# A top-k attention and PReLU MLP kernel: where the copy of an output block and the transposes of q and k stand in their queues

## The chip, the cores and the metric

The kernel runs on one core of one Trainium2 chip. The metric is the device time of one execution in microseconds (us). A core has five engines, each with a queue of its own that it works off in order: TensorE (PE in the profile), VectorE (DVE), ScalarE (ACT), GpSimd (POOL) and SyncE (SP, which only issues DMAs here). They wait for each other through semaphores.

## The reference: what is computed

For 8 batches of 8 heads, with 576 rows of 64 numbers each, attention is computed in which each row keeps only its 32 largest scores:

```python
scores = scale * np.matmul(q, k.transpose(0, 1, 3, 2))
kth = np.partition(scores, -32, axis=-1)[..., -32:-31]
scores = np.where(scores >= kth, scores, -1e9)
attn = np.exp(scores - np.max(scores, axis=-1, keepdims=True))
attn = attn / (np.sum(attn, axis=-1, keepdims=True) + 1e-09)
x = np.matmul(attn, v)            # then (B, S, H*D) -> (4608, 512)
h = x @ w_in                      # (512, 2048)
g = np.maximum(h, 0.0) + alpha * np.minimum(h, 0.0)
out = g @ w_out                   # (2048, 512)
```

q, k, v, weights and output are float32. The output is 4608 rows of 512: 36 blocks of 128 rows.

## The kernel before, in words

**Units of work.** Heads are handled in 32 pairs, 4 pairs a batch. The rows of scores are cut into 144 duos: a duo is two tiles of 128 rows by 576 scores (lines 77 to 85). A batch is 18 duos: 16 of kind "n" (a tile of each head of a pair) and 2 of kind "m" (the last 64 rows of the heads, put together). The main loop (line 722) has one slot for each duo and 4 more to drain. Everything in flight is shifted against the duo whose scores are made: in slot n

- PE makes the scores of duo n+1 into the only `ps_sc` buffer (`st_qk`, line 233), and the products of attention weights and v for duo n-7 into `xo` (`st_av`, line 429);
- ACT runs two Sign passes with counts for duo n-2 (`sg`, `st_count`), Exp for duo n-5 (`w`, `st_exp`), two Relu passes for duo n-4 (`r`, `st_relu`), and copies the scores of duo n+1 from `ps_sc` to `s_sb` (`st_exit`, line 255), which frees `ps_sc`;
- POOL multiplies scores by signs (`y`), then subtracts the Relu result from the scores (`s_sb<-s_sb,r`), and casts v;
- DVE takes the largest 8 of six groups a row (12 instructions `up` and `small`), every second slot folds them into a threshold `p`, takes row maxima of `y` into `p`, picks the threshold for Relu (`KZ`), and normalises `xo` (a reciprocal into `KZ`, then `x`);
- SP transposes the weights of Exp by DMA (`wT<-w`) and issues the loads and stores.

**The MLP** is spread over the slots. When 128 or 256 transposed tokens (`xT`) are there, units of h are put into a list (`mlp_ready`, line 510). A unit (`h_pe`, line 547) is 8 or 16 products into `ph`; DVE turns it into `gT` with a maximum (`h_dve`, line 566). The linear share of the activation is handled by a weight matrix `w_lin_b` made once (the "lin" items of slots 16 to 23). An output block of 128 tokens is four parts (`part`, line 532), numbered 0 to 3, of one product with `w_lin_b` and four with `w_out_b`, all into the only `pz` buffer. `o_pe` (line 572) issues the next part, but only when no finished block waits for its copy (`not stores`). Part 3 puts the block on `stores`, with the first slot in which it may be copied: `now[0] + late_o[0]`. `o_act` (line 577) is the copy `o_sb<-pz` on ACT; the DMA to memory is issued by SP at the beginning of the next slot (`o_sp`, line 591; by POOL in three slots of the drain).

**q and k of later pairs** are loaded to staging buffers, transposed on PE in three units (`prep_pe`, line 186): four 128x128 transposes of k, four of q, and two of the tails of both, into a `tps` buffer. `tps`, `ph` and the filler products share a pool of two buffers (`ps_h`, tag "h"). The transposes are copied to `qkT` at the end of the slot (lines 767 to 771): the wide ones of k, in even slots, on DVE, those of q, in odd slots, on ACT, the tails on DVE. From pair 4 on, a pair's three units stand in three slots that follow each other, and the fourth slot has none.

**The order in a slot** is written by hand; the engines keep the order of the program. On PE in slot n: a unit of h or, if there is none, four filler products on an idle tile (`keep_warm`, `rest<-idle`, line 560); scores of duo n+1; av; a part of a block (line 745); in some even slots a second unit of h; transposes (line 756); then a second part if more than two are ready (line 763), or a filler if no part ran. On ACT: Sign twice, Exp, Relu twice, the copy of the scores, then `o_act` (line 758), then the copy of q's transposes. `o_act` runs if the kernel is in the drain, if more than 4 parts are ready, or if only short copies of transposes are pending in this slot. `late_o` is 1 only around the second part (line 762 to 766): a block that ends in the first part of a slot may be copied in that same slot, one that ends in the second part in the next.

The helper at line 32 records every instruction, so the profile gives "L32" for all of them; they are told apart by the names of their tiles.

Of the kernel before, what the change touches and what calls it, by code (L numbers as in the profile page):

```python
# [59 lines left out]
def fast_path(tc, q, k, v, moe_w_in, moe_w_out, moe_alpha, out, flag):  # L60
# [27 lines left out]
    with ExitStack() as ctx:  # L88
# [89 lines left out]
        todo, now = {}, [0]  # L178
# [5 lines left out]
        pend = []  # L184
# [44 lines left out]
        def two_of(ap, step, m):  # L229

            return bass.AP(ap.tensor, ap.offset, [list(ap.ap[0]), [step, 2], [1, m]])

        def st_qk(n):

            d = duos[n]
            ps = ps_s.tile([128, 1536], FP32, name="ps_sc", tag="s")
            T["ps", n] = ps
            if d[0] == "n":  # L240
                _, p, j = d
                t = qkT[p]
                c = slice(128 * j, 128 * j + 128)
                PE.matmul(ps[:, 0:512], t[0:64, 1, c], t[0:64, 0, 0:512], start=True, stop=True)
                PE.matmul(ps[:, 1024:1536], t[64:128, 1, c], t[64:128, 0, 64:S], start=True, stop=True)
                PE.matmul(two_of(ps[:, 512:1024], 448, 64), t[:, 1, c],
                          kds[p % len(kds)].rearrange("p (a b) -> p a b", a=2), start=True, stop=True)
                return
            for i, o, n0, n1 in ((0, 0, 0, 512), (1, 960, 64, S), (0, 0, 512, S), (1, 960, 0, 64)):
                t = qkT[d[1 + i]]  # L250
                for h in range(2):
                    r = slice(64 * h, 64 * h + 64)
                    PE.matmul(ps[r, o + n0:o + n1], t[r, 1, 512:S], t[r, 0, n0:n1], start=True, stop=True)

        def st_exit(n):
            s = s_p.tile([128, 2, S], FP32, name="s_sb", tag="s")
            ACT.copy(s, two_of(T.pop(("ps", n)), 960, S))
            T["s", n] = s
# [119 lines left out]
        def duos_at(kind, n):  # L378
            return stage.get((kind, n), [])
# [15 lines left out]
        def st_count(n):  # L395
            s, p9 = T["s", n], T["p9", n // 2]
            sg = two.tile([128, 2, S], BF16, name="sg", tag="sg", bufs=3)
            if n % 2 == 0:
                T["cs", n // 2] = three.tile([128, 4], FP32, name="cs", tag="cs")
            cs = T["cs", n // 2]  # L400
            for i in range(2):
                r = 2 * (n % 2) + i
                ACT.activation(sg[:, i, :], s[:, i, :], AF.Sign, bias=p9[:, r, 0:1], scale=-1.0,
                               accum_out=cs[:, r:r + 1])
            T["sg", n] = sg
# [16 lines left out]
        def st_exp(n):  # L422
            w = ws[n % 3]
            ACT.activation(w[:, :, 0:S], T.pop(("s", n)), AF.Exp, scale=att_scale)
            wt = three.tile([128, 10, 128], BF16, name="wT", tag="wT")
            SP.dma_start_transpose(wt, w.rearrange("p a b -> p (a b)"))
            T["wt", n] = wt

        def st_av(n):
            d = duos[n]  # L430
            wt = T.pop(("wt", n))
            if n % 2 == 0:
                T["xo", n // 2] = ps_x.tile([128, 2, 2, 65], FP32, name="xo", tag="x")
            xo = T["xo", n // 2][:, n % 2, :, :]
            for i in range(2):
                if d[0] == "n":
                    p = d[1]
                    for c in range(5):
                        K = 128 if c < 4 else 64
                        PE.matmul(xo[:, i, :], wt[0:K, 5 * i + c, :], v1[p][0:K, c, i, :],  # L440
                                  start=(c == 0), stop=(c == 4))
                else:
                    p = d[1 + i]
                    for h in range(2):
                        for c in range(5):
                            K = 128 if c < 4 else 64
                            PE.matmul(xo[64 * i:64 * i + 64, h, :], wt[0:K, 5 * i + c, 64 * h:64 * h + 64],
                                      v1[p][0:K, c, h, :], start=(c == 0), stop=(c == 4))
# [59 lines left out]
        soon, hq, oq, act, stores, late_o = [], [], [], [], [], [0]  # L508
# [38 lines left out]
        def h_pe(most=1):  # L547
            while soon and soon[0][0] <= now[0]:
                hq.append(soon.pop(0)[1])
            if hq and wi_free and len(act) < most:  # L550
                hq.pop(0)()
                return True

        def ready():
            k = 0
            while lin_done and k < len(oq) and oq[k][0]["done"] >= oq[k][1]:
                k += 1
            return k

        def keep_warm():  # L560

            ps = ps_h.tile([128, 512], FP32, name="rest", tag="h")
            for i in range(4):
                PE.matmul(ps, idle[:, 0:128], idle, start=(i == 0), stop=(i == 3))
# [7 lines left out]
        def o_pe():  # L572
            if ready() and not stores:
                oq.pop(0)[2]()
                return True

        def o_act():

            if stores and stores[0][3] <= now[0]:
                z, t0, pieces, _ = stores.pop(0)  # L580
                o = io.tile([128, DMODEL], FP32, name="o_sb", tag="io")
                ACT.copy(o, z)
                at, left = 0, []
                for r0, m in pieces:
                    if t0 <= at < t0 + 128:
                        left.append((r0, at - t0, m))
                    at += m
                outs.append((o, left))
        outs = []

        def o_sp():
            while outs:
                o, left = outs.pop(0)
                for r0, p, m in left:
                    (POOL if now[0] in (ND + 1, ND + 2, ND + 3) else SP).dma_start(out[r0:r0 + m, :], o[p:p + m, :])
# [74 lines left out]
        def run(n, kind, most=99):  # L670
            l = todo.get((n, kind), [])
            for f in l[:most]:
                f()
            if l[most:]:
                todo.setdefault((n + 1, kind), [])[0:0] = l[most:]
# [46 lines left out]
        for n in range(ND + 4):  # L722
            end = n >= ND
            now[0] = n
            run(n, "ld")
            o_sp()

            if end:
                for m in duos_at("av", n):
                    st_av(m)  # L730
            if not h_pe() and not end:
                keep_warm()
            if n and on(n + 1):
                st_qk(n + 1)
            if not end:
                for m in duos_at("av", n):
                    st_av(m)
            late = len(hq) > (9 if n < 118 else 4) and n % 2 == 0 or end

            for m in duos_at("count", n):  # L740
                st_count(m)
                st_y(m)
            for m in duos_at("exp", n):
                st_exp(m)
            did = o_pe()
            run(n, "w")

            dve_slot(n, late)
            for m in duos_at("relu", n):
                st_relu(m, 0)  # L750
                st_relu(m, 1)
            if on(n + 1):
                st_exit(n + 1)
            run(n, "cast")
            run(n, "lin_out")
            run(n, "prep", 2 if n < 4 else 1)
            if end or ready() > 4 or all(len(d.shape) == 3 for d, _ in pend):
                o_act()
            if (n, "lin") in todo:
                run(n, "lin")  # L760
            else:
                late_o[0] = 0 if end else 1
                if not (end or ready() > 2) or not o_pe():
                    if not end and not did:
                        keep_warm()
                late_o[0] = 0
            while pend:
                short = len(pend[0][0].shape) == 3
                wide = pend[0][0].shape[1] == 512
                on_dve = short and n > 16 or wide and (n < 17 or n % 2 == 0)  # L770
                prep_evac(DVE.tensor_copy if on_dve else ACT.copy)
            if n == 1:
                sm(DVE.tensor_copy(alpha_ps, aps), [], [(304, 320)])
                ACT.activation(alpha1m, aps, AF.Copy, scale=-1.0, bias=1.0)
            run(n, "scale")
            if norm_of(n):
                st_xT(norm_of(n) - 1)
                st_xT(norm_of(n))
            if n == ND + 3:
                check_low()  # L780
# [294 lines left out]
```

## Time and profile before

| | |
|---|---|
| median of 3 runs | 869.93 us (868.83 to 876.24) |
| the profiled execution | 875.8 us, of which the span from first to last instruction is 873.7 us |
| mean granted clock of PE | 0.956 |
| busy: PE, DVE, ACT, POOL | 773.5, 763.8, 766.2, 755.4 us |
| loop, 121 to 813 us: busy DVE, ACT, POOL | 642.7, 645.1, 639.8 of 692 us |

In a row of the timeline the first number is the start in us from the span's start, the second the duration; then follow engine, line, operation, the tile written, the tile read, shapes and the number of instructions merged. Brackets at the end give the idle time of the engine just before, and what ended it. Durations on one engine overlap a little, as instructions are pipelined, so the step from one start to the next is what counts. A row of the waits gives: who waited, for whom, us in total, how many times, the longest. A row of the table by stage gives the stretch, its length, the busy time and instructions of PE, PEld (weight loads), DVE, ACT and POOL, the granted clock of PE as a share of full speed, the busy share of the DMA engines and GB/s.

### The profile page before, as it was taken

The page shows a single profiled execution, that of the slowest core. Times are in us where ns is not written, and L with a number is a line of the kernel's source. Part 1 is how long each engine was busy: PE and PEld are TensorE (multiplying, and loading weights), DVE is VectorE, ACT ScalarE, POOL GpSimd, SP SyncE. Part 2 cuts the span into 40 slices and gives each one's busy share as a digit, 9 for nine tenths or more (in the row PEclk, how much of TensorE's full clock was granted, in tenths as well). Part 3 has the DMA queues.
Part 4 walks back from the last instruction along what each step waited for, and adds up shares of the span by engine and source line. Part 5 has one row for each costly group of instructions (what it writes and reads, how often), then busy time and mean ns, then how long its engine had stood idle before and what let it go on. Part 6 is the DMA issues. An engine that isn't in the chain of part 4 may idle for free.

```text
span 873.7 us, 17781 instructions
## 1 busy us (share of the span) xinstructions
PE 773.5 (89%) x5386; PEld 434.0 (50%) x5386; DVE 763.8 (87%) x3475; ACT 766.2 (88%) x1255; POOL 755.4 (86%) x708
## 2 busy tenths in 40 slices
PE   8778799989988989899978999989879889899887
PEld 5333345555545555455544555555445555455454
DVE  4879889999998999989998898999897889999732
ACT  4789999999997999989998899999997888999830
POOL 2789989999997898989997898999897987999930
PEclk9979899999999999989989999999998999999989
DMA  7599976555564455545555455556756554344341
GB/s 145 145 174 171 170 140 133 114 115 104 130 125 102 100 118 118 113 112 104 130 117 110 103 110 119 116 125 119 124 107 112 109 93 96 77 91 77 79 97 41
DMA packets 344167, 100.19 MB, mean 115 GB/s; under 512 B 338032, under 2 KB 338048, under 8 KB 344064
## 3 DMA queue, kind: packets, MB, share of 16 engines
q1 hardware_dynamic: 340992, 91.87, 53.3%
q0 software_dynamic: 1872, 6.82, 3.3%
q8 instruction: 44, 0.72, 0.3%
q14 instruction: 59, 0.48, 0.2%
q10 hardware_dynamic: 1200, 0.30, 0.2%
HBM read 36.71 MB, written 9.44 MB: 53 GB/s over the span
## 4 chain that ended last, share of the span: by engine, by line
PE 41%; ACT 21%; DVE 18%; POOL 8%; issue 7%; DMA 4%; SPq 0%; ACTq 0%; POOLq 0%; DVEq 0%
PE pz L32 13%; PE ps_sc L32 11%; PE ph L32 7%; ACT sg L32 6%; ACT r L32 6%; DVE small L32 6%; PE xo L32 5%; ACT s_sb L32 5%; POOL y L32 4%; DVE p L32 4%; POOL s_sb L32 4%; DVE up L32 3%; ACT w L32 3%; DMA wT<-w 3%; PE rest L32 2%
## 5 line engine op out<-in xcount | busy, mean ns | idle before, releaser
L32 POOL TENSOR_TENSOR y<-s_sb,sg 128x576 f32<-128x576 f32 x288 | 362.1, 1278 | 81.6 <-ACT sg L32 80.8
L32 POOL TENSOR_TENSOR s_sb<-s_sb,r 128x576 f32<-128x576 f32 x288 | 362.0, 1278 | 2.1 <-ACT r L32 2.0
L32 ACT ACTIVATE sg<-s_sb,p 128x576 bf16<-128x576 f32 x288 | 221.0, 771 | 10.4 <-DVE p L32 9.4
L32 DVE MAX8 p<-y 128x8 f32<-128x576 f32 x288 | 215.2, 748 | 7.5 <-POOL y L32 6.8
L32 DVE MAX8 up<-s_sb 128x8 f32<-128x96 f32 x864 | 211.9, 245 | 9.4 <-ACT s_sb L32 9.0
L32 DVE MAX8 small<-s_sb 128x8 f32<-128x96 f32 x864 | 216.0, 250 | 0.0
L32 ACT ACTIVATE r<-s_sb,KZ 128x576 bf16<-128x576 f32 x288 | 205.8, 764 | 0.6 <-DVE KZ L32 0.6
L32 PE MATMUL ps_sc<-qkT 64*128 64x512 f32 (+2 forms) x768 | 184.3, 578 | 21.1 <-ACT s_sb L32 20.7
L32 ACT COPY s_sb<-ps_sc 128x1152 f32<-128x1152 f32 x144 | 159.1, 1105 | 45.6 <-PE ps_sc L32 45.3
L32 ACT ACTIVATE w<-s_sb 128x1152 bf16<-128x1152 f32 x144 | 166.1, 1153 | 5.3 <-POOL s_sb L32 5.0
L32 PE MATMUL ph<-xT,w_in_b 128*128 128x256 bf16 (+1 forms) x1408 | 158.6, 263 | 1.6 <-ACT qkT L32 1.0
L32 PE MATMUL pz<-w_out_b,gT 128*128 128x512 bf16 x576 | 158.0, 398 | 2.3 <-DVE gT L32 2.3
L32 PEld LDWEIGHTS <-w_in_b 128*128 128x128 bf16 x1408 | 123.9, 102 | 43.2 <-issue 11.1
L32 PE MATMUL xo<-v,wT 128*128 128x65 bf16 (+3 forms) x1600 | 127.4, 199 | 8.4 <-DMA wT<-w 8.3
L32 DVE TENSOR_SCALAR gT<-ph 128x512 bf16<-128x512 f32 x144 | 97.5, 678 | 30.5 <-PE ph L32 30.2
L32 PEld LDWEIGHTS <-wT 128*128 128x128 bf16 (+3 forms) x1600 | 98.2, 100 | 38.1 <-DMA wT<-w 8.9
L32 PEld LDWEIGHTS <-gT 128*128 128x128 bf16 x576 | 57.8, 101 | 106.0 <-issue 53.3
L32 PE MATMUL pz<-w_lin_b,xT 128*128 128x512 bf16 x144 | 57.2, 397 | 44.1 <-ACT o_sb L32 44.1
L32 PEld LDWEIGHTS ps_sc<-qkT 64*128 64x128 f32 (+1 forms) x768 | 53.9, 172 | 79.3 <-issue 35.9
L32 PEld LDWEIGHTS ps_sc<-kd,qkT 128*128 128x128 f32 x256 | 38.3, 189 | 99.1 <-issue 99.1
L32 PE MATMUL rest<-idle 128*128 128x512 bf16 x228 | 62.7, 405 | 11.2 <-DVE gT L32 7.8
L32 PE MATMUL ps_sc<-kd,qkT 128*128 128x128 f32 x256 | 62.8, 327 | 0.0
(57 smaller groups left out, 574.7 us busy)
## 6 DMA issues: line engine op xcount, KB each, us to landing
k_st<-in_k_dram SPq DMA_DIRECT2D x64, 128.0 KB, 2.8
v_st<-in_v_dram SPq DMA_DIRECT2D x64, 128.0 KB, 2.8
q_st<-in_q_dram SPq DMA_DIRECT2D x62, 128.0 KB, 2.8
out_dram<-o_sb SPq DMA_DIRECT2D x31, 256.0 KB, 2.5
w_st<-in_moe_w_out_dram POOLq DMA_DIRECT2D x4, 1024.0 KB, 7.0
wT<-w SPq DMA_TRANSPOSE x144, 3.5
w_in_b<-in_moe_w_in_dram POOLq DMA_DIRECT2D x4, 512.0 KB, 6.6
k_st<-in_k_dram SPq DMA_DIRECT2D x32, 32.0 KB, 2.6
```

The costliest lines, as they stand in the source:

```text
L32: ins = self.tc.keep_in_program_order(f(*a, **kw))
```

## The change

Three things move; no arithmetic changes.

- The copy of an output block (`o_act`) stands right behind Exp, ahead of the two Relus and of the copy of the scores. Its condition is now: the drain, or more than 4 parts ready, or no wide copy of transposes on ACT in this slot (`wide_copy`: an odd slot with transposes).
- `late_o` is set to 1 ahead of the first part and stays so through the loop: a block is copied at the earliest in the slot behind its last product. As before, no part is issued while a finished block waits.
- From slot 4 on the transposes of a slot are issued on PE right behind the unit of h, ahead of the scores (in slots 0 to 3 behind the scores). Their copies stay at the end of the slot.

In the order of instructions that follows, there are 36 copies and 36 x 4 parts as before; 34 copies stand in a slot with a part 0 (23 before); fillers are 56 groups of four products (57 before); in the drain POOL issues one store (3 before) and SP the others; after the slots, one part more is left to do.

```diff
             if not h_pe() and not end:
                 keep_warm()
+            wide_copy = n % 2 and (n, "prep") in todo
+            if n > 3:
+                run(n, "prep", 1)
             if n and on(n + 1):
                 st_qk(n + 1)
+            if n < 4:
+                run(n, "prep", 2)
             if not end:
                 for m in duos_at("av", n):
                     st_av(m)
...
             for m in duos_at("exp", n):
                 st_exp(m)
+            late_o[0] = 0 if end else 1
+            if end or ready() > 4 or not wide_copy:
+                o_act()
             did = o_pe()
             run(n, "w")
...
             run(n, "cast")
             run(n, "lin_out")
-            run(n, "prep", 2 if n < 4 else 1)
-            if end or ready() > 4 or all(len(d.shape) == 3 for d, _ in pend):
-                o_act()
             if (n, "lin") in todo:
                 run(n, "lin")
             else:
-                late_o[0] = 0 if end else 1
                 if not (end or ready() > 2) or not o_pe():
                     if not end and not did:
                         keep_warm()
-                late_o[0] = 0
```

## The prediction

> **What bounds the kernel now.** I read the page first (engines, clock, chain), then the waits between 120 and 813 us (the steady loop), then the busy table by stage, and last the timelines of TensorE (PE) and ScalarE (ACT) around the copies.
>
> ```profile
> span 873.7 us, 17781 instructions
> PE 773.5 (89%) x5386; PEld 434.0 (50%) x5386; DVE 763.8 (87%) x3475; ACT 766.2 (88%) x1255; POOL 755.4 (86%) x708
> PE 41%; ACT 21%; DVE 18%; POOL 8%; issue 7%; DMA 4%; SPq 0%; ACTq 0%; POOLq 0%; DVEq 0%
> ```
>
> Four engines are busy for 86 to 89%, and the chain changes between them: no single one is the bound, so the question is what makes all of them wait. Who waits for whom in the loop (us in total, times, longest):
>
> ```profile
> POOL y L32 <- ACT sg L32: 51.5, 47, 3.5
> PE pz L32 <- ACT o_sb L32: 39.8, 18, 3.2
> ACT s_sb L32 <- PE ps_sc L32: 29.6, 25, 3.3
> DVE KZ L32 <- PE xo L32: 18.1, 19, 2.0
> ACT sg L32 <- DVE p L32: 8.9, 11, 1.3
> DVE qkT L32 <- PE tps L32: 4.2, 11, 0.5
> ACT o_sb L32 <- PE pz L32: 4.2, 7, 0.6
> ```
>
> The second line is the one that the change touches: the first product of an output block (pz) waits 18 times, 2.2 us each, for ACT to copy the block before it out of the only pz buffer. The third is ACT waiting for the scores (ps_sc), so PE, stopped by ACT, stops ACT in turn. Stages side by side (busy us of PE, PEld, DVE, ACT, POOL, then the granted clock):
>
> ```profile
> 121.00:813.00 692.00, 626.32 (x4403) 354.68 (x4400) 642.68 (x2967) 645.12 (x1053) 639.76 (x576) 0.97 0.55 111
> 534.80:613.70 78.90, 72.70 (x524) 41.47 (x522) 77.04 (x358) 77.32 (x127) 76.37 (x70) 1.00 0.57 115
> 394.40:452.30 57.90, 50.92 (x369) 29.19 (x367) 56.64 (x263) 57.12 (x94) 57.15 (x53) 1.00 0.58 120
> 736.00:813.40 77.40, 70.55 (x524) 39.26 (x522) 74.36 (x350) 76.45 (x126) 76.13 (x66) 1.00 0.44 88
> 452.30:530.00 77.70, 69.06 (x483) 39.33 (x482) 68.76 (x318) 68.49 (x113) 69.29 (x63) 0.91 0.55 111
> ```
>
> Three clean stretches run ACT at 98.0, 98.7 and 98.8% (77.32/78.9, 57.12/57.9, 76.45/77.4) at full clock; in a disturbed one it is at 88% (68.49/77.7) at clock 0.91. What opens a disturbance:
>
> ```profile
> 453.94 0.59 PE L32 MATMUL pz<-w_lin_b,xT 128*128 128x512 bf16 x1 [3.22 <-ACT o_sb L32]
> 454.32 1.91 PE L32 MATMUL pz<-w_out_b,gT 128*128 128x512 bf16 x4
> ...
> 524.51 0.58 PE L32 MATMUL pz<-w_lin_b,xT 128*128 128x512 bf16 x1 [2.28 <-ACT o_sb L32]
> ```
> ```profile
> 460.76 1.12 ACT L32 COPY s_sb<-ps_sc 128x1152 f32<-128x1152 f32 x1 [2.96 <-PE ps_sc L32]
> 466.73 1.12 ACT L32 COPY s_sb<-ps_sc 128x1152 f32<-128x1152 f32 x1 [0.95 <-PE ps_sc L32]
> ```
>
> PE idles 3.22 us; the products behind it then take 1.91 us for four where an undisturbed four takes 1.02 (next fence): PE comes back at about half rate. After 2.28 us the first product takes 0.58, after 1.94 it takes 0.38 (next fence): the limit lies between. The scores are late twice, and ACT loses 2.96 + 0.95 = 3.9 us. So a wait costs more than itself.
>
> [...]
>
> **The change part by part.** One slot in full, from PE and from ACT:
>
> ```profile
> 410.67 1.03 PE L32 MATMUL ph<-xT,w_in_b 128*128 128x256 bf16 x8
> 411.63 1.13 PE L32 MATMUL ps_sc<-qkT 64*128 64x512 f32 x4
> ...
> 413.02 0.78 PE L32 MATMUL xo<-v,wT 128*128 128x65 bf16 x10
> 413.73 0.66 PE L32 MATMUL tps<-ident_f,q_st 128*128 128x128 f32 x4
> 416.32 0.38 PE L32 MATMUL pz<-w_lin_b,xT 128*128 128x512 bf16 x1 [1.94 <-ACT o_sb L32]
> 416.54 1.02 PE L32 MATMUL pz<-w_out_b,gT 128*128 128x512 bf16 x4
> 417.40 1.04 PE L32 MATMUL ph<-xT,w_in_b 128*128 128x256 bf16 x8
> ```
> ```profile
> 409.77 1.10 ACT L32 COPY s_sb<-ps_sc 128x1152 f32<-128x1152 f32 x1
> ...
> 412.30 1.16 ACT L32 ACTIVATE w<-s_sb 128x1152 bf16<-128x1152 f32 x1
> 413.36 1.42 ACT L32 ACTIVATE r<-s_sb,KZ 128x576 bf16<-128x576 f32 x2
> 414.69 1.09 ACT L32 COPY s_sb<-ps_sc 128x1152 f32<-128x1152 f32 x1
> 415.69 0.58 ACT L32 COPY o_sb<-pz 128x512 f32<-128x512 f32 x1
> ```
>
> (1) The copy moves from behind the slot's s_sb copy to behind Exp (w). Exp gives way at 413.36, so the copy would stand there, 2.33 us before 415.69, and end at 413.94. PE reaches the block's first product at 413.73 plus the transposes moved ahead, at most 0.66: 414.39. The wait of 1.94 goes to nothing here. It is a PE wait, so it is worth what it costs ACT, DVE and POOL later, not 39.8 us. ACT's own work is unchanged: 36 copies before, 36 after, of 0.58 us. Both Relus (r) and the s_sb copy of such a slot come up to 0.58 later, the next Sign does not. Who waits for Relu is POOL's subtraction, but POOL does y first; in the loop its wait is for sg (51.5), and that view has none for r, so I take 0 (bounds: 0, and 0.58 x 36 = 21 us if POOL had no slack).
>
> (2) A block is copied a slot after its last product (late_o is 1 throughout). So ACT no longer waits for that product: 4.2 us in 7 waits go. Of the 36 copies, 34 are followed by the next block's first product in the same slot (23 before), so more of them can wait for Exp. An undisturbed PE would start the scores when the s_sb copy ends, 409.77 + 1.10 = 410.87, spend 411.63 to 413.73 = 2.10 on scores and av, and stand at 412.97; the copy ends at 413.94: 1.0 us of idle, which by the 1.94 above costs no clock. The new condition lets a copy stand in the slot of a pair's first transposes and keeps it out of the odd slot of the second, where ACT makes the wide transposes' copy: a block is then copied a slot later, and PE runs a filler meanwhile. SP issues the store at the next slot's start as before, when its copy has been done for 2 us longer; it delays no transposing DMA behind it.
>
> (3) The transposes (tps) of slots 4 and up move ahead of the scores. PE's sum is the same. h, scores, av and one part of a block take 0.96 + 2.10 + 1.08 = 4.14 (differences of the starts above), with wide transposes at most 4.80, against an ACT slot of 414.69 - 409.77 = 4.92. Two parts: 5.22 without transposes, against 4.92 + 0.58 = 5.50 in a slot with a copy. The scores take 413.02 - 411.63 = 1.39, and ACT wants them at 414.69, 3.82 after 410.87: they may start 2.4 us late before ACT notices. So PE fits. DVE's copy of the transposes no longer waits for them: up to 4.2 us of DVE. Against that, av comes up to 0.66 later for the reciprocal (KZ), which waits 18.1 now; they are waits for a late PE, which (1) relieves, so 0 net (bounds -4 and +8, 0.66 x 12).
>
> (4) What the transposes now wait for: the tps buffer is one of two shared with h, so the second unit of a pair (q) waits for the copy of the first, which ends DVE's slot:
>
> ```profile
> 410.92 0.68 DVE L32 COPY qkT<-tps 128x512 f32<-128x512 f32 x1
> ```
> ```profile
> 492.61 0.69 DVE L32 COPY qkT<-tps 128x512 f32<-128x512 f32 x1 [0.47 <-PE tps L32]
> ```
> ```profile
> 490.43 1.12 ACT L32 COPY s_sb<-ps_sc 128x1152 f32<-128x1152 f32 x1 [0.21 <-PE ps_sc L32]
> ```
>
> It ends 0.75 us after ACT's s_sb copy in a clean slot (411.60 against 410.87) and 1.75 in a late one (493.30 against 491.55). With 0.66 of transposes the scores start 1.4 to 2.4 us after ACT's slot: just inside the 2.4. Queued behind are scores, av and the block's part; ACT and DVE wait for those. Cost 0, cover 0 to 1.0 us; if the cover is gone, the s_sb copy is late next (rival A).
>
> (5) Loads: the staging loads keep their slots on SP (2.8 us to landing, issued three slots of 4.9 us ahead), so transposes a slot's length earlier still find them. Stores stay 37 + 3 in number; two more go from SP instead of POOL at the end, hidden behind products. Four fewer filler products (rest): nothing.
>
> **The sum.** Loop work on ACT is 645.12. At the clean stretches' mean, 210.89/214.2 = 98.45%, the loop takes 655.3 instead of 692: -36.7 (bounds: 98.0% gives -33.7; ACT without any idle -46.9). Ahead of the loop ACT waits for scores, so transposes ahead of them cost one unit, +0.7 (bounds 0 and 1.4):
>
> ```profile
> 109.22 1.12 ACT L32 COPY s_sb<-ps_sc 128x1152 f32<-128x1152 f32 x1 [0.87 <-PE ps_sc L32]
> ```
>
> In the drain the new order leaves one more part behind PE's last slot, and one first product straight behind its copy: 417.40 - 416.32 = 1.08 and 0.58 by the rows above, +1.7 (upper bound too; lower -1.5, if the 3.17 us wait there goes):
>
> ```profile
> 827.52 0.38 PE L32 MATMUL pz<-w_lin_b,xT 128*128 128x512 bf16 x1 [3.17 <-ACT o_sb L32]
> ```
>
> 875.8 (the profiled execution: span 873.7 and 2.1 around it) - 36.7 + 0.7 + 1.7 = 841.5. The runs' median, 869.93, lies 5.9 below that execution. Part of that spread should be the half-rate stretches themselves, which the change takes away; I carry half of it over: 841.5 - 3.0 = 838.5.
>
> **Rivals.** A, slower: the wait moves into (4). If PE idles some 2 us between h and the q transposes, the clock halves there: 24 pairs in the loop, 3.9 us each by the two s_sb rows above. From 12 of 24 the kernel is slower by over 1% (36.7 + 8.7 = 45.4, over 3.9); all 24 would give 838.5 + 94 = 932. For it: the late copies (1.75 us behind ACT). Against: most of that lateness follows the disturbances, and clean copies end at 0.75. Chance 0.11.
>
> [...]
>
> B, half: the first product now waits for Exp in 34 slots, most of them even, where Sign can wait for DVE's threshold (8.9 us in 11 waits, to 1.3). 1.0 + 1.3 = 2.3 us of idle throttles in some. Half the gain stays: 838.5 + 18 = 857. Chance 0.17.
>
> C, no change: the loop is held by the ring Sign, y, row maximum, threshold, Sign, and the PE waits only filled its slack: 870. Against: POOL waits 51.5 us for Sign, and the clean stretches show the ring at 98%. Chance 0.06.
>
> **How the numbers follow.** Forecast 0.66, on its own range 828 (98.8%, drain -1.5, all of the 5.9, rounded) to 845 (98.0%, nothing carried over). With B the range is 827 to 860; it leaves out A, C and the edges. A measurement of this kernel tells about 1% from no change (861.2 to 878.6 counts as the same). Faster: forecast and nearly all of B, 0.81; the same: C and the rest of B, 0.08; slower: A, 0.11.
>
> **What would show it.** Right: pz waiting for o_sb falls from 39.8 to under 15 us in the loop with none over 2; clock in 121 to 813 at 0.99 or 1.00; s_sb waiting for ps_sc from 29.6 to under 8; ACT at 98% of a loop near 655 us; new waits of tps for qkT under 1 us each. Wrong: half-rate products behind q transposes (A); clock still 0.97 with pz waits over 2 us (B); sg waiting for p grown to 30 us or more (C).

## The result and the profile after

The changed kernel takes 842.71 us (median of 4 runs, 840.79 to 850.75) against 871.14 beside it: a ratio of 0.9684, 95% interval 0.9606 to 0.9761. Measured once more later, it took 838.92 against 872.49: 0.9606, interval 0.9574 to 0.9638. It is faster by 3 to 4%. The profiled execution took 840.79 us.

The page of the changed kernel, span and engines:

```profile
span 839.0 us, 17803 instructions
PE 751.4 (90%) x5382; PEld 426.0 (51%) x5382; DVE 759.2 (90%) x3475; ACT 763.5 (91%) x1255; POOL 753.7 (90%) x706
```

ACT, DVE and POOL do the same work (763.5, 759.2 and 753.7 us, within 4.6 us of before) in a span 34.7 us shorter. The waits of the changed kernel from 120 to 780 us, which is its loop (us in total, times, longest):

```profile
PE pz L32 <- ACT o_sb L32: 13.6, 19, 1.2
POOL y L32 <- ACT sg L32: 11.2, 14, 2.1
DVE KZ L32 <- PE xo L32: 5.9, 7, 1.2
ACT sg L32 <- DVE p L32: 5.7, 11, 0.8
POOL s_sb L32 <- ACT r L32: 5.6, 15, 0.4
ACT s_sb L32 <- PE ps_sc L32: 5.1, 5, 2.1
```

The first product of a block waits as often as before (19 times, 18 before) but 0.7 us instead of 2.2, never over 1.2. ACT's wait for scores fell from 29.6 to 5.1, DVE's for av from 18.1 to 5.9, POOL's for Sign from 51.5 to 11.2: that these are echoes of the first is what the experiments test. One wait is new: POOL for Relu, 5.6 us in 15 waits. The same 657 us of the table by stage, the kernel before first, the changed kernel second (PE, PEld, DVE, ACT, POOL, clock):

```profile
121.00:778.00 657.00, 594.16 (x4147) 335.78 (x4144) 607.93 (x2805) 610.96 (x997) 605.98 (x548) 0.96 0.56 113
```
```profile
121.00:778.00 657.00, 606.56 (x4419) 347.71 (x4416) 638.22 (x2967) 643.48 (x1054) 639.71 (x576) 1.00 0.59 117
```

ACT is busy for 97.9% instead of 93.0%, and the clock is 1.00 instead of 0.96. The slot that held the 3.22 us wait before, now, on ACT:

```profile
438.37 1.15 ACT L32 ACTIVATE w<-s_sb 128x1152 bf16<-128x1152 f32 x1
439.42 0.56 ACT L32 COPY o_sb<-pz 128x512 f32<-128x512 f32 x1
439.88 1.44 ACT L32 ACTIVATE r<-s_sb,KZ 128x576 bf16<-128x576 f32 x2
441.23 1.10 ACT L32 COPY s_sb<-ps_sc 128x1152 f32<-128x1152 f32 x1
```

and on PE:

```profile
438.37 0.78 PE L32 MATMUL xo<-v,wT 128*128 128x65 bf16 x10
440.03 0.38 PE L32 MATMUL pz<-w_lin_b,xT 128*128 128x512 bf16 x1 [0.88 <-ACT o_sb L32]
440.25 1.02 PE L32 MATMUL pz<-w_out_b,gT 128*128 128x512 bf16 x4
```

The copy gives way 1.35 us before the copy of the scores begins, where it used to stand behind it. PE waits 0.88 us and goes on at full rate: 1.02 for the four products that took 1.91.

### The profile page after: what moved, and what is told of

The parts are those of the page before. It is cut to its first block, busy times and chain, and to the rows that moved or that the text cites. A ratio compares the mean times of both kernels' runs of the same rounds, so it can differ in the third digit from the quotient of the medians.

```text
span 839.0 us, 17803 instructions
## 1 busy us (share of the span) xinstructions
PE 751.4 (90%) x5382; PEld 426.0 (51%) x5382; DVE 759.2 (90%) x3475; ACT 763.5 (91%) x1255; POOL 753.7 (90%) x706
## 4 chain that ended last, share of the span: by engine, by line
DVE 38%; POOL 19%; ACT 17%; PE 15%; issue 6%; DMA 3%; SPq 0%; ACTq 0%; POOLq 0%
DVE small L32 11%; DVE p L32 10%; POOL y L32 9%; POOL s_sb L32 9%; DVE up L32 7%; DVE gT L32 5%; ACT r L32 5%; ACT sg L32 5%; PE ps_sc L32 4%; ACT s_sb L32 4%; PE pz L32 3%; ACT w L32 3%; PE ph L32 3%; PE rest L32 2%; DMA wT<-w 2%
## 5 line engine op out<-in xcount | busy, mean ns | idle before, releaser
L32 PE MATMUL ph<-xT,w_in_b 128*128 128x256 bf16 (+1 forms) x1408 | 150.8, 255 | 5.3 <-ACT qkT L32 2.9
L32 PE MATMUL pz<-w_out_b,gT 128*128 128x512 bf16 x576 | 148.8, 381 | 0.3 <-DVE gT L32 0.3
L32 PEld LDWEIGHTS <-w_in_b 128*128 128x128 bf16 x1408 | 119.2, 99 | 48.7 <-issue 12.0
L32 PE MATMUL xo<-v,wT 128*128 128x65 bf16 (+3 forms) x1600 | 127.0, 199 | 11.2 <-DMA wT<-w 11.2
L32 PEld LDWEIGHTS <-wT 128*128 128x128 bf16 (+3 forms) x1600 | 97.9, 100 | 40.3 <-DMA wT<-w 11.8
L32 PEld LDWEIGHTS <-gT 128*128 128x128 bf16 x576 | 55.9, 98 | 71.9 <-issue 16.9
L32 PEld LDWEIGHTS ps_sc<-qkT 64*128 64x128 f32 (+1 forms) x768 | 56.0, 170 | 64.4 <-ACT s_sb L32 30.3
```

The lines of the kernel that those rows point to most:

```text
L32: ins = self.tc.keep_in_program_order(f(*a, **kw))
```

## The experiments

The theory: the change gains because the first product no longer waits over about 2 us, so TensorE comes neither late nor at half rate (1.91 us instead of 1.02 for four products) to the next scores. The rivals: the earlier transposes gain; the clock is incidental; every microsecond of the wait costs the same. `late_o` needs no run of its own: in the change the copy stands ahead of both places where a part is issued, so a block that ends in a slot can't be copied before the next slot, whatever `late_o` is in the loop.

**The copy alone.** The transposes go back behind av and the first part:

```diff
-            if n > 3:
-                run(n, "prep", 1)
...
-            if n < 4:
-                run(n, "prep", 2)
...
             run(n, "lin_out")
+            run(n, "prep", 2 if n < 4 else 1)
```

> The copy behind Exp and late_o as in the change, the transposes at their old place behind av and the first part. Theory 1 (the change gained because the first product no longer waits over 2 us, so TensorE is neither late nor throttled): nearly the whole gain is here, 840 to 850 us against 871, loop clock 0.99 or more, pz waiting for o_sb under 20 us in the loop. Rival (the earlier transposes made the gain, since VectorE no longer waits for them): 860 us or more, and VectorE still waits some 4 us for tps.

Measured: 843.07 us, ratio 0.9674 (0.9642 to 0.9707). Its waits in the loop and its row by stage:

```profile
PE pz L32 <- ACT o_sb L32: 15.1, 20, 1.2
ACT s_sb L32 <- PE ps_sc L32: 2.4, 4, 1.0
DVE qkT L32 <- PE tps L32: 1.8, 5, 0.5
```
```profile
121.00:778.00 657.00, 602.14 (x4330) 346.79 (x4396) 637.55 (x2960) 643.13 (x1050) 639.21 (x575) 1.00 0.60 117
```

The whole gain is here. VectorE's waits for transposes fell by themselves, from 4.2 to 1.8 us, while ACT's for them rose from 1.1 to 3.5; what moved them is not shown.

**The transposes alone**, the copy left where it was:

```diff
             if not h_pe() and not end:
                 keep_warm()
+            if n > 3:
+                run(n, "prep", 1)
             if n and on(n + 1):
                 st_qk(n + 1)
+            if n < 4:
+                run(n, "prep", 2)
...
-            run(n, "prep", 2 if n < 4 else 1)
```

> The transposes ahead of the scores as in the change, the copy at its old place behind the copy of the scores. Theory 1: no gain, 866 to 885 us; the first product still waits for the copy, by some 0.3 us longer each time because the transposes no longer stand in the gap; loop clock 0.97 or lower. Rival (transposes): 840 to 850 us.

Measured: 871.32 us, ratio 0.999 (0.9961 to 1.0018).

```profile
PE pz L32 <- ACT o_sb L32: 37.4, 17, 3.2
ACT s_sb L32 <- PE ps_sc L32: 34.7, 30, 2.6
```
```profile
121.00:778.00 657.00, 585.06 (x4079) 335.12 (x4140) 605.98 (x2804) 610.35 (x996) 605.64 (x549) 0.96 0.56 113
```

Both waits stay, and so does the clock of 0.96. VectorE's wait for the transposes (4.2 us before) is not among the waits of this run, and yet nothing is gained. This part of the change is worth nothing that can be measured. The longer gap that the expectation allowed for didn't show in the longest wait (3.2 as before).

**The clock by itself.** The kernel before, with four filler products ahead of the first product in the 19 slots in which it follows the copy. The copy and the block's order stay:

```diff
+                held = len(stores)
                 o_act()
+                if len(stores) < held and not end and ready() > 2:
+                    keep_warm()
```

> The kernel before, with four filler products ahead of the first product in the 19 slots in which it follows the copy; the copy and the wait for it stay where they were. Theory 1, part of the clock: the waits named for pz are cut by the fillers' 0.9 us but the first product starts no earlier; TensorE keeps its full rate (loop clock 0.99 or more), the scores are late less often (s_sb waiting for ps_sc under 15 us instead of 29.6), 848 to 860 us. Rival (the clock is incidental, the late first product itself makes the loss): 866 to 874 us, s_sb waiting for ps_sc near 30 us.

Measured: 857.99 us, ratio 0.9861 (0.9812 to 0.991).

```profile
PE rest L32 <- DVE gT L32: 17.8, 24, 2.0
ACT s_sb L32 <- PE ps_sc L32: 15.7, 14, 2.6
PE pz L32 <- ACT o_sb L32: 13.2, 14, 1.7
```
```profile
121.00:778.00 657.00, 600.44 (x4247) 343.36 (x4312) 620.99 (x2872) 624.13 (x1020) 619.58 (x559) 0.99 0.58 115
```

The first product still waits for the same copy; only a part of the gap ahead of it is filled with work that nobody needs (fillers themselves wait 17.8 us for a buffer that VectorE frees, 7.8 in the kernel before). The clock rises from 0.96 to 0.99, the scores' lateness halves (29.6 to 15.7), and 1.4% come back, a third to a half of the change's gain of 3.2 to 3.9%. So the clock is not incidental. Whether the rest belongs to the late product itself is not shown, as slow stretches remain. This is one of them; another, at 643.34, is alike:

```profile
446.03 1.02 PE L32 MATMUL rest<-idle 128*128 128x512 bf16 x4 [1.17 <-DVE gT L32]
448.08 0.59 PE L32 MATMUL pz<-w_lin_b,xT 128*128 128x512 bf16 x1 [1.03 <-ACT o_sb L32]
448.46 1.92 PE L32 MATMUL pz<-w_out_b,gT 128*128 128x512 bf16 x4
```

Neither gap is over 1.2 us, but they follow each other closely: 2.2 us of idle with one group of fillers between.

**One step later.** The changed kernel with the copy behind the first Relu, and then behind both. The number of ready parts is taken where it was, so the parts keep their slots. The first of the two:

```diff
-            if end or ready() > 4 or not wide_copy:
-                o_act()
-            did = o_pe()
+            rd = ready()
+
+            def copy_and_part():
+                if end or rd > 4 or not wide_copy:
+                    o_act()
+                return o_pe(rd)
+            if end:
+                did = copy_and_part()
...
+            for m in relus:
                 st_relu(m, 0)
+                if not end and m == relus[0]:
+                    did = copy_and_part()
                 st_relu(m, 1)
```

In the second, `copy_and_part()` stands behind this loop.

> The change, with the copy one step later: behind the first Relu (0.7 us behind Exp). Theory 1 with a limit near 2 us: the first product's waits grow to some 1.6 us each and cost nothing, since the scores have slack and the clock stays: 839 to 847 us, pz waiting for o_sb 25 to 40 us in the loop, loop clock 0.99 or more. Rival (each microsecond of that wait costs in proportion; 2.33 us of earlier copy brought 29 us): 0.7/2.33 x 29 = 9 us slower than the change, 850 us or more.

Measured: 845.5 us, ratio 0.9713 (0.9679 to 0.9748).

```profile
PE pz L32 <- ACT o_sb L32: 24.4, 23, 1.9
ACT s_sb L32 <- PE ps_sc L32: 8.3, 11, 1.7
```
```profile
605.21 0.38 PE L32 MATMUL pz<-w_lin_b,xT 128*128 128x512 bf16 x1 [1.55 <-ACT o_sb L32]
...
631.16 0.58 PE L32 MATMUL pz<-w_lin_b,xT 128*128 128x512 bf16 x1 [1.55 <-ACT o_sb L32]
```

Little is lost: 2.4 us against the copy alone, measured beside it, and 3 to 7 against the two measurements of the change; the clock in 121 to 778 us is 0.99. But two equal waits of 1.55 us end differently: full rate behind one, a slow product behind the other. There is no sharp limit near 2 us.

> The change, with the copy behind both Relus (1.4 us behind Exp; in five slots with a second unit of h that unit also goes ahead of the part). In the changed kernel the first product waits up to 0.9 us in an undisturbed slot, so here some 2.3 us, at the limit that the trace before gave (1.94 kept the rate, 2.28 did not). Theory 1: the half rate comes back in part, loop clock 0.97 to 0.99, s_sb waiting for ps_sc 10 to 25 us, 850 to 862 us. Rival (each microsecond of the wait costs the same, as the step to the first Relu, 2 to 3 us for 0.7, would have it): 5 us above the change, 846 to 849 us.

Measured: 860.51 us, ratio 0.9863 (0.9828 to 0.9899).

```profile
PE pz L32 <- ACT o_sb L32: 38.9, 24, 2.5
ACT s_sb L32 <- PE ps_sc L32: 19.6, 19, 2.2
```
```profile
121.00:778.00 657.00, 598.29 (x4251) 341.39 (x4251) 621.41 (x2875) 625.87 (x1022) 622.79 (x561) 0.97 0.58 115
```

The second 0.7 us cost 15 us, the first 2 to 7, so a price in proportion to the wait is out. Note the total: 38.9 us of this wait, about as in the kernel before (39.8), and yet the run is 1.4% faster. Its waits are shorter, 1.6 us on average and 2.54 at most instead of 2.2 and 3.22; that this is the reason is argued.

**Back behind the copy of the scores**, with late_o and the transposes as in the change:

```diff
             if on(n + 1):
                 st_exit(n + 1)
+            if not end:
+                did = copy_and_part()
```

> The change, with the copy behind the copy of the scores, where it stood before; late_o and the transposes stay as in the change. Theory 1: waits of about 3 us, half rate behind most of them, all of the gain gone: 864 to 880 us, loop clock 0.97 or lower. Rival (in proportion, 2.4 us for 0.7): 2.4 us later costs 8 us, about 851 us. Second rival (copying a block a slot later is what gains, not the place in the slot): 840 to 850 us.

Measured: 902.98 us, ratio 1.0333 (1.0299 to 1.0367): slower than the kernel before, more than any theory had given.

```profile
PE pz L32 <- ACT o_sb L32: 64.8, 27, 3.5
ACT s_sb L32 <- PE ps_sc L32: 59.7, 38, 4.5
```
```profile
121.00:778.00 657.00, 577.32 (x3996) 326.96 (x3996) 585.45 (x2695) 587.66 (x961) 583.68 (x529) 0.94 0.55 110
```

Against the transposes alone, which have the copy at the same place, the slot of the copy is the main difference (its condition is that of the change, and in a few slots a second unit of h goes ahead of the part): a copy a slot later has the next block's first product in its own slot in 34 cases instead of 23, so 27 waits instead of 17, 59.7 us of late scores instead of 34.7, and a clock of 0.94. "One slot behind" is thus no gain in itself; the place behind Exp makes up for it.

**The same for the linear weights.** The four copies `w_lin_b<-plin` move behind Exp too:

```diff
             run(n, "w")
+            run(n, "lin_out")
...
-            run(n, "lin_out")
```

> The change, and the four copies of the linear weights (w_lin_b, slots 18 to 24) moved behind Exp in the same way. TensorE's order stays the same. Theory 1 carried to another buffer: plin waits 4.0 us for w_lin_b in the changed kernel, and the scores are late 3.7 us in four slots behind; both go, 838 to 842 us against the change's 843. Rival (that stage is held by TensorE's own work): no difference.

Measured: 837.44 us, ratio 0.9585 (0.9558 to 0.9613). The wait that goes, in the changed kernel:

```profile
PE plin L32 <- ACT w_lin_b L32: 4.0, 3, 1.6
```

It is not among the waits of this run, and ACT's wait for scores falls to 2.9 us. Whether that is worth time is told by the last group.

**Fewer fillers at the start**, on top of it:

```diff
-            if not h_pe() and not end:
+            if not h_pe() and not end and n not in (8, 16, 17, 18, 19):
...
-                    if not end and not did:
+                    if not end and not did and n not in (7, 15):
```

> The run before (copies of the linear weights behind Exp), and without the fillers at the end of slots 7 and 15 and at the beginning of slots 8 and 16 to 19, where TensorE comes late from a wait for wT and the scores are late behind the fillers (3.22, 1.01 and 1.41 us). Theory: the scores come up to 3 us earlier in slot 8 and 1 to 2 us in slots 16 and 17, 834 to 839 us. Rival (without fillers the clock stays at half for longer and takes it back): no difference or slower.

Measured: 836.56 us, ratio 0.9573 (0.9549 to 0.9597): no difference. The copy of the scores in slot 8 of the run before, and then of this one:

```profile
62.89 1.12 ACT L32 COPY s_sb<-ps_sc 128x1152 f32<-128x1152 f32 x1 [3.46 <-PE ps_sc L32]
```
```profile
61.31 1.12 ACT L32 COPY s_sb<-ps_sc 128x1152 f32<-128x1152 f32 x1 [2.10 <-PE ps_sc L32]
86.91 1.12 ACT L32 COPY s_sb<-ps_sc 128x1152 f32<-128x1152 f32 x1 [1.87 <-PE ps_sc L32]
```

1.4 us less are waited in slot 8; a new wait of 1.87 stands at 87 us. That fits the rival (less work, half rate for longer), and the mean granted clock is a little lower (0.975 to 0.979 over the executions of this run, 0.978 to 0.983 in the run before), but the rate was not tested by itself there, and the profiled execution of this run took 844.88 us, 8 more than its median, so the new wait may belong to that execution alone.

**Side by side on one chip.** The change again; both copies behind Exp with the transposes at their old place (the diffs of the copy alone and of the linear weights together); the change with the linear weights' copies behind Exp, again.

> The changed kernel itself, once more, on the same chip as the next two: 840 to 845 us, 0.965 to 0.970 of the kernel before.

> Both copies behind Exp (output block and linear weights), the transposes at their old place behind av. If the transposes' move is worth nothing also there: within 2 us of the next run, 836 to 840 us. If it brings what the prediction allowed it, VectorE's 4 us of waits: 840 us or more, 3 us or more above the next run.

> The change with the copies of the linear weights behind Exp, once more, beside the change itself: 836 to 840 us, 4 to 6 us under the change, if the gain seen on another chip is one of the kernel; no difference if it was one of the chip.

Measured: 838.92 (0.9606, 0.9574 to 0.9638), 840.03 (0.9618, 0.9586 to 0.965) and 838.46 (0.961, 0.9578 to 0.9643). The three agree. So the 5 us of the linear weights' copies are not shown to be the kernel's; they came with another measurement, its chip or chance, and no version here is shown to beat the change. The transposes' move shows no worth here either: 1.6 us between the second and the third, inside the intervals.

## Why the prediction was right, point by point

**The wait at the copy, (1) and (2).** Right. 1.0 us of idle was worked out for an undisturbed slot; the slot shown has 0.88, and no wait in the loop is over 1.2. The copy alone brings the whole gain. ACT's 4.2 us of waiting for the block's last product are gone from the waits. Relu's delay was priced at nothing: POOL does wait for Relu now, 5.6 us in 15 waits, far from the bound of 21. Whether these waits cost time was not tested; they are 5.6 us at most.

**The wait costs more than itself.** Right in kind: the fillers show the clock's part, the two steps behind Relu that the price isn't proportional. The limit "between 1.94 and 2.28" was a misreading: it rests on two waits, and others of the same trace, the kernel before, already speak against it. One of 1.72 us ended in slow products, one of 2.31 did not:

```profile
681.05 0.59 PE L32 MATMUL pz<-w_lin_b,xT 128*128 128x512 bf16 x1 [1.72 <-ACT o_sb L32]
681.42 1.91 PE L32 MATMUL pz<-w_out_b,gT 128*128 128x512 bf16 x4
...
757.95 0.38 PE L32 MATMUL pz<-w_lin_b,xT 128*128 128x512 bf16 x1 [2.31 <-ACT o_sb L32]
758.16 1.02 PE L32 MATMUL pz<-w_out_b,gT 128*128 128x512 bf16 x4
```

In the experiments one wait of 1.55 us ended in a slow product (above), and the one of 2.54 us, in the run with the copy behind both Relus, did not:

```profile
483.99 0.38 PE L32 MATMUL pz<-w_lin_b,xT 128*128 128x512 bf16 x1 [2.54 <-ACT o_sb L32]
```

Counted over the loops, with the four products behind the first one included: none of the 19 waits of the changed kernel (up to 1.20 us) was followed by slow products, 4 of the 11 waits of 1.49 to 1.87 us in the run behind the first Relu, 7 of the 10 of 2.15 to 2.94 us in the kernel before, and both of its 3.22 us. So the waits of the changed kernel cost no clock (1.00 in the loop), as forecast, but not because of a limit above 1.94. For the same cause the one wait of 1.94 us behind transposes, with its 1.02 for the four, doesn't settle what such a wait costs: one of 2.15 us behind the same transposes, at 371.24 us of the same trace, was followed by four products in 1.91.

What makes equal waits end differently was not shown. The run with the copy behind both Relus has no such wait over 2.54 us in the loop, and a clock of 0.97.

**The transposes, (3) and (4).** Right that they net to nothing: 0.999 alone, nothing measurable on top of the copy. PE has new gaps ahead of them (the rows below, for weight loads and products, changed kernel, 120 to 780 us; the profile names no engine that ended them), all under 2 us, with a loop clock of 1.00; so rival A did not come about.

```profile
PEld tps L32 <- issue: 11.6, 17, 1.7
PE tps L32 <- issue: 7.8, 6, 1.5
```

**The sum.** The copies of the scores that open and close the loop, before, then after:

```profile
120.96 1.10 ACT L32 COPY s_sb<-ps_sc 128x1152 f32<-128x1152 f32 x1
...
813.37 1.12 ACT L32 COPY s_sb<-ps_sc 128x1152 f32<-128x1152 f32 x1
```
```profile
121.62 1.10 ACT L32 COPY s_sb<-ps_sc 128x1152 f32<-128x1152 f32 x1
...
778.70 1.10 ACT L32 COPY s_sb<-ps_sc 128x1152 f32<-128x1152 f32 x1
```

Loop: 692.41 to 657.08, -35.3 (predicted -36.7). Start: +0.66 (predicted +0.7), which is luck: in the run of the copy alone, with the transposes at their old place, the same copy begins at 123.38 us. Drain: 873.7 - 813.37 = 60.3 before, 839.0 - 778.70 = 60.3 after, 0 (predicted +1.7; inside its bounds). The sum made 841.5 for the profiled execution; it took 840.79. That closeness is in part luck: the profiled execution before lay 3 to 5 us above the medians of its kernel (871.14 to 872.71), the one after 1.9 below the median of its four runs, and the medians differ by 28 to 34 us, not by 35. What missed is the 3.0 us carried over from the median's distance: with more runs the kernel before stood at 871 to 873, so the distance of 5.9 was in part a chance of three runs, and the rest was no hint of a faster after. In the first measurement 838.5 was 4.2 us too low; in the second it was met to 0.4, and the two differ by as much. The lower end of the range, 828, is a little off its own terms: 645.12/0.988 is a loop of 653.0, and with the start at 0 they add up to 829.4.

**The rivals.** B's gap of 2.3 us did not arise: Sign's wait for the threshold fell too (8.9 to 5.7 us, 0.8 at most), and no wait for the copy is over 1.2. The copy behind both Relus has waits of the size that B had in mind, and took 860.5 (B's forecast: 857). C is out: with the first product's wait gone, the ring runs at 98%.

## What to carry to other kernels

A copy that frees TensorE's only accumulator belongs at the point of the copying engine's queue at which TensorE arrives, not at the end of its turn (here 843.07 us with the copy behind Exp, 872.46 in the kernel before); work out both times from the starts in one slot. Judge such a wait by its longest cases and by the granted clock of the stage, and not by its total alone: here 39 us of it in waits of up to 2.5 us took 18 us longer than 14 us of it did, and 40 us in waits of up to 3.2 us took 28 us longer. If the wait must stay, filler products in the gap can help; here they brought back a third to a half.

## What the runs showed of the hardware that was not expected

TensorE came back at about half rate from some idle gaps under 2 us, and the length of one gap doesn't decide it: four products that take 1.02 us at full rate took 1.91 behind a gap of 1.72 us in the kernel before, and 1.03 behind one of 2.54 in the run with the copy behind both Relus. What came just before seems to count too. In the filler run 1.17 and 1.03 us of idle, with one group of fillers between, were followed by four products in 1.92. In the run with the copy behind both Relus two waits of 0.99 us (at 404.04 and 601.90 us) were followed by four products in 1.79 and 1.68 us; both stood behind the twenty av products of an "m" duo, whose rows say 128*64 where others say 128*128. Whether these products are the reason was not tested.

Copying a block a slot later with the copy at its old place cost about 30 us (902.98 against 871.32, each beside a kernel before of 872.5 to 872.7) though no work was added: ten more waits of the kind went with it.
